# An attention-and-gate kernel on one core: TensorE's order for batches 1 to 3 written by slots, and batch 0's first stage in two parts

## Chip, core and metric

The kernel runs on one core of a Trainium2 chip. The metric is the device time of one execution in microseconds (us); lower is better. The engines are TensorE (PE), VectorE (DVE), ScalarE (ACT), GpSimd (POOL) and SyncE (SP), the last of which here only issues loads. Each engine carries out its own row of instructions in order.

## What is computed

Two layers in a row, on x of 4 batches, 12800 positions and 128 channels, with 32 inducing vectors. All arrays are float32, the three weights float64 on the host's side, and cut to what matters the reference is:

```python
def mab(q, kv):                      # scale = 1 / sqrt(128)
    s = scale * (q @ kv.transpose(0, 2, 1))
    s = s - s.max(-1, keepdims=True)
    a = np.exp(s)
    a /= a.sum(-1, keepdims=True) + 1e-09
    return a @ kv
h = mab(I, x)                        # 32 x 128 a batch: every position of x is read
x = mab(x, h)                        # back to 12800 x 128
# then, with a causal convolution of 5 taps a channel:
gate = 1.0 / (1.0 + np.exp(-gate_pre))   # gate_pre[t] = sum_k conv_w[k] * x[t - 4 + k]
val = x @ w_val
return gate * val @ w_out
```

The second layer's output of `mab` is a mixture of only 32 rows of h. The kernel therefore multiplies h by the taps and by w_val once a batch, and gets gate and value straight from the attention weights.

## The kernel before

A batch is cut into seven units: six of 4 x 512 positions and one of 4 x 128, which is unit 0 in batch 0 and unit 6 in the others (`units`). Its work has two stages.

**Stage 1** makes h. For each unit a load brings xT (channels by positions); TensorE multiplies it by the inducing vectors (`a_mm`, L280, four column tiles side by side), VectorE takes the maximum (`a_max`, L284) and transposes the scores into the tile e (`a_tr`, L289). When all seven units are there, `p_ml` to `p_mc` (L294 to L313) make one maximum of them: VectorE, TensorE, VectorE, TensorE, VectorE in turn. Then come the subtraction (`a_sub`, L318), the exp (`a_exp`, L323), the sum z (`a_z`, L335 or L342) and the product h (`a_h`, L353), which needs x with positions first, the tile xk. Batches 1 to 3 load xk, subtract and sum on GpSimd. Batch 0 makes xk by TensorE transposes (`a_kt`, L256, 100 of them) and ACT copies (`a_ke`, L269), and subtracts on VectorE. `p_z` to `p_hq` make the h weights hq. From these `p_v` to `p_we` make, on TensorE and in some 15 small VectorE steps, the stacked weights wstk (float16 in two parts) and wo.

**Stage 2** makes the outputs, unit by unit: scores against hq (`b_mm`, L456, psum tile of one buffer, tag s), transposition, row maximum, subtraction on GpSimd, exp on ACT, sum, normalizing on GpSimd, transposition back (`b_tr` to `b_back`, L461 to L493). Then it splits into two float16 parts (`b_hi` on ACT, `b_lo` on GpSimd with the four positions before each strip, L499 to L511). The **gate** is 60 row-tiled matmuls into two psum tiles g0 and g1 of one buffer each (`c_gate`, through `strips`, L520), then two tanh on ACT (`c_tanh`, L531). The **value** is 12 more matmuls into the same two psum tiles (`c_val`); VectorE multiplies value and gate (`c_gv`, L541, twice a unit), TensorE multiplies by wo (`c_out`, L546, four a unit, psum tag o with two buffers), ACT copies out (`c_ev`, L553) and stores.

In batch 3 the value is issued in two halves, the first after the first tanh (`PAIRS`); in the other batches it is issued whole, after both.

**What sets the order.** The program is not written in order. `stage1` and `stage2` hand each step to a list (`Plan.add`) with an engine, a planned duration, a key and the steps it needs; `Plan.order` then takes again and again, on the engine whose best step can start first, the step of the lowest key among those that can start within SLACK (0.17 us) of the earliest. The keys are linear in unit and batch: KEY1 for stage-1 scores, KEYH for h, KEYP for the steps on h, and in `stage2` the unit's number, less KS for the steps ahead of the gate. The resulting rows are static; nothing is chosen on the chip. Loads are one chain on SP's queue: all xT loads of a batch, then all its xk loads (batch 0 has none of these), then the next batch. xT has 12 buffers, freed by `b_mm`; xk has four, freed by `a_h`. The three weights are loaded on ACT's queue (`weights`, L194 to L196).

## Time and profile before

| | before |
|---|---|
| median of three runs | 338.98 us (338.87 to 339.67) |
| the profiled execution | 338.89 us |
| its span, first to last instruction | 337.1 us |
| mean granted TensorE clock | 0.975 |
| TensorE busy | 313.0 us |
| outputs (L546), 128x512 | 192 matmul instructions, 629 ns each |
| gate and value (L520), 512 wide | 1728 matmuls, 375 ns each |
| SP's queue, xT loads of 1 MB | 24, median 10.8 us to landing |

A float32 matmul is two instructions in the trace, so one output is x2 and the four scores of a unit are x8; a group of row-tiled or column-tiled matmuls runs side by side, and the times of single instructions in it overlap. In a row of the timeline stand start, length, engine, line, operation, output, inputs, shapes and count, and in brackets the idle time before it with what ended it. The ends of matmuls are modelled, so I read TensorE's costs from start to start. Weight loads (PEld) have a row of their own.

### The profile page before, as it was taken

To read this page: it belongs to the slowest core of one execution; us is meant where nothing else is said; L and a number is where in the kernel's file an instruction comes from. 1 tells how busy PE (TensorE), PEld (TensorE's weight loads), DVE (VectorE), ACT (ScalarE), POOL (GpSimd) and SP (SyncE) were. 2 spreads that over 40 slices of the span, in tenths; PEclk is the share of its full clock that TensorE was granted. 3 is DMA by queue.
4 is the path that set the end of the run, shared out by engine and by line. 5 is a ranking of instruction groups with operands and counts; after the bars stand their busy time and mean duration, and the time that the engine had idled before them with its cause. 6 is when DMAs were issued, how large, how long until landed. Compare 5 with 4: busy or idle time off the path is not lost.

```text
span 337.1 us, 9075 instructions
## 1 busy us (share of the span) xinstructions
PE 313.0 (93%) x3874; PEld 136.3 (40%) x3874; DVE 207.6 (62%) x412; ACT 171.2 (51%) x270; POOL 148.4 (44%) x244
## 2 busy tenths in 40 slices
PE   2999787999599999999799999999999999999993
PEld 0767623334343333334334333444443443333341
DVE  1578587845348867962756797844557878643220
ACT  1458032655334553576364354675643655665562
POOL 0000048349753223689683126899640376551000
PEclk9999859999989999999999999999999999999997
DMA  7997096008991638929984659763333140333324
GB/s 297 419 416 305 7 384 269 33 0 325 420 405 40 221 126 287 422 104 365 386 318 184 249 185 379 267 253 142 126 126 124 64 189 33 126 125 122 125 116 172
DMA packets 11475, 72.96 MB, mean 216 GB/s; under 512 B 1285, under 2 KB 1578, under 8 KB 2986
## 3 DMA queue, kind: packets, MB, share of 16 engines
q1 hardware_dynamic: 7056, 45.88, 35.2%
q10 hardware_dynamic: 4378, 26.50, 19.8%
q8 instruction: 30, 0.49, 0.6%
q14 instruction: 11, 0.09, 0.1%
HBM read 46.16 MB, written 26.21 MB: 215 GB/s over the span
## 4 chain that ended last, share of the span: by engine, by line
PE 85%; DMA 6%; DVE 3%; ACT 2%; POOL 1%; issue 1%; SPq 0%; ACTq 0%; POOLq 0%
PE g L520 30%; PE o L546 27%; PE s L280 7%; PE s L456 7%; PE h L353 7%; DMA xT<-in_xt_dram 5%; PE gp L256 4%; DMA ind<-in_inducing_dram 1%; PE wt L441 1%; POOL hl L504 1%; ACT gt L531 1%; ACT os L553 0%; DVE z L481 0%; PE zp L335 0%; PE t L308 0%
## 5 line engine op out<-in xcount | busy, mean ns | idle before, releaser
L520 PE MATMUL g<-hl,wstk 32*128 32x512 f16 (+1 forms) x2016 | 110.3, 352 | 0.5 <-ACT gt L531 0.5
L546 PE MATMUL o<-gt,wo 128*128 128x512 f32 (+1 forms) x224 | 105.6, 582 | 1.1 <-ACT os L553 0.6
L541 DVE SCALAR_TENSOR_TENSOR gt<-gt,g 128x1024 f32<-128x1024 f32 (+1 forms) x56 | 59.5, 1098 | 44.2 <-PE g L520 44.0
L553 ACT COPY os<-o 128x512 f32<-128x512 f32 (+1 forms) x112 | 59.2, 541 | 53.6 <-PE o L546 53.0
L520 PEld LDWEIGHTS <-wstk 32*128 32x128 f16 x2016 | 45.9, 92 | 75.6 <-issue 35.3
L531 ACT ACTIVATE gt<-g,gsc 128x1024 f32<-128x1024 f32 (+1 forms) x56 | 54.2, 1018 | 39.4 <-PE g L520 39.4
L471 POOL TENSOR_TENSOR q<-q,m 128x512 f32<-128x512 f32 (+1 forms) x28 | 26.8, 955 | 74.3 <-DVE m L466 73.7
L546 PEld LDWEIGHTS o<-gt,wo 128*128 128x128 f32 x224 | 35.4, 190 | 49.9 <-issue 29.8
L488 POOL TENSOR_TENSOR q<-q,z 128x512 f32<-128x512 f32 (+1 forms) x28 | 26.8, 956 | 51.5 <-DVE z L483 39.0
L504 POOL TENSOR_TENSOR hl<-p,hl 128x512 f16<-128x512 f32 (+1 forms) x28 | 29.6, 1057 | 21.3 <-ACT hl L499 21.0
L280 PE MATMUL s<-xT,iw 128*32 128x512 f32 (+1 forms) x224 | 28.5, 587 | 8.3 <-DMA xT<-in_xt_dram 5.8
L456 PE MATMUL s<-xT,hq 128*32 128x512 f32 (+1 forms) x224 | 30.0, 610 | 1.6 <-DVE hq L384 1.2
L284 DVE TENSOR_REDUCE nm<-s 128x1 f32<-128x512 f32 (+1 forms) x28 | 17.6, 627 | 21.0 <-PE s L280 21.0
L353 PE MATMUL h<-xk,e 128*32 128x128 f32 x800 | 28.2, 281 | 0.0
L318 POOL TENSOR_TENSOR e<-e,mb 128x512 f32<-128x512 f32 (+1 forms) x21 | 24.1, 1156 | 7.7 <-DVE mb L313 6.8
L499 ACT CAST hl<-p 128x512 f16<-128x512 f32 (+1 forms) x28 | 16.1, 575 | 22.3 <-DVE p L493 20.5
L353 PEld LDWEIGHTS h<-xk,e 128*32 128x32 f32 x800 | 21.9, 112 | 12.6 <-issue 5.7
L476 ACT ACTIVATE q<-q 128x512 f32<-128x512 f32 (+1 forms) x28 | 16.4, 586 | 20.6 <-POOL q L471 20.1
L481 DVE TENSOR_REDUCE z<-q 128x16 f32<-128x512 f32 (+1 forms) x28 | 17.3, 616 | 12.2 <-ACT q L476 12.1
L461 DVE STREAM_TRANSPOSE q<-s 128x512 f32<-128x512 f32 (+1 forms) x28 | 18.1, 647 | 8.2 <-PE s L456 8.2
L493 DVE STREAM_TRANSPOSE p<-q 128x512 f32<-128x512 f32 (+1 forms) x28 | 17.9, 641 | 8.0 <-POOL q L488 7.8
L342 POOL TENSOR_TENSOR za<-za,e 128x512 f32<-128x512 f32 (+1 forms) x18 | 20.5, 1141 | 2.1 <-ACT e L323 1.7
(88 smaller groups left out, 210.5 us busy)
## 6 DMA issues: line engine op xcount, KB each, us to landing
xT<-in_xt_dram SPq DMA_DIRECT2D x24, 1024.0 KB, 10.8
out_dram<-os ACTq DMA_DIRECT2D x24, 1024.0 KB, 4.4
xk<-in_xk_dram SPq DMA_DIRECT2D x18, 1024.0 KB, 8.5
xT<-in_xt_dram SPq DMA_DIRECT2D x4, 256.0 KB, 3.2
out_dram<-os ACTq DMA_DIRECT2D x4, 256.0 KB, 2.2
xk<-in_xk_dram SPq DMA_DIRECT2D x3, 256.0 KB, 4.9
raw<-in_moe_w_val_dram ACTq DMA_DIRECT2D x1, 128.0 KB, 7.6
raw<-in_moe_w_out_dram ACTq DMA_DIRECT2D x1, 128.0 KB, 10.0
```

What stands on the lines that cost most here:

```text
L280: T.matmul(sc[M * g:M * g + M, :w], c_["iw"], x[:, w * g:w * g + w], start=True, stop=True, tile_position=(0, M * g))
L318: (V if MADE(b) else Gp).tensor_tensor(e[:, :n], e[:, :n], bat[b]["mb"].broadcast_to([P, n, M]), ALU.subtract)
L353: T.matmul(d["h"][M * s:M * s + M, :P], e[:, i, :], x[i], start=v == 0 and i < G, stop=v == NU - 1 and i >= n - G, tile_position=(0, M * s))
L456: T.matmul(sc[M * g:M * g + M, :w], bat[b]["hq"], x[:, w * g:w * g + w], start=True, stop=True, tile_position=(0, M * g))
L471: Gp.tensor_tensor(q[:, :n], q[:, :n], st[b, u, "m"][:, :n].broadcast_to([P, n, M]), ALU.subtract)
L488: Gp.tensor_tensor(q[:, :n], q[:, :n], st[b, u, "z"][:, :n].broadcast_to([P, n, M]), ALU.mult)
L504: Gp.tensor_tensor(h[:, 1, 4:4 + w], st[b, u, "p"][:, :w], h[:, 0, 4:4 + w], ALU.subtract)
L520: T.matmul(bank[g // 2][:, g % 2, :w], wst[s, wp, k, :], h[s, part, 4 - d:4 - d + w], start=first and i == 0, stop=last and i == 2, tile_p ...
L531: S.activation(t[:, :, :w], st[b, u, "g"][i][:, :, :w], AF.Tanh, scale=bat[b]["gsc"])
L541: V.scalar_tensor_tensor(t[:, :, :w], t[:, :, :w], 1.0, st[b, u, "g"][i][:, :, :w], ALU.add, ALU.mult)
L546: T.matmul(op[:, :w], bat[b]["wo"], st[b, u, g // 2, "t"][:, g % 2, :w], start=True, stop=True)
L553: S.copy(os[:, w * g:w * g + w], st[b, u, g, "o"][:, :w])
```

## The change

What it does, part by part:

- **TensorE's order from slot 7 on** (a slot is one unit's gate and what follows up to the next gate; slot = 7 x batch + unit). Tables give each step a slot: S1AT for stage-1 scores, HAT for h, S2AT for stage-2 scores, MAXAT, HQAT, PVAT and WTAT for the small steps, EARLY for how many outputs of the unit before stand ahead of the value. Within a slot the places are: gate; weight copies; stage-1 scores; stage-2 scores; h; early outputs; value; remaining outputs. `at` records them, and at the end every step is made to need the one ahead of it. Up to slot 6 the planner still chooses, with new keys from the same tables, a wider SLACK, and a planned price for leaving a shape (SHAPE, LEAVE, KEEP).
- **The value is issued whole in batch 3 too** (PAIRS is false).
- **Psum:** stage-1 scores always use tag o, so s serves stage-2 scores alone; some small tiles and the second weight copy of a batch move to o.
- **Batch 0's stage 1 in two parts:** units 1 to 4, then 5, 6 and 0. Each part has its own maximum, sum and h; the first is subtracted on GpSimd, the second on VectorE. The new functions q_f to q_hq scale and join the two.
- **Batch 0's units 5 and 6 load xk** in place of transposing (68 transposes stay).
- **Loads:** xT and xk become two chains that the planner weaves together; the weights go to the head of SP's queue.
- Batch 0's weight copies take two wider steps in place of three.

The core of the diff (the tables' numbers but for a few left out; the new functions q_z, q_rz, q_hs and q_hc are a few VectorE steps on 32 columns each):

```diff
 def PAIRS(b):
-    return b == 3
+    return False
 def TAG1(b, u):
-    return "o" if b == 0 or b == 1 and u < 2 else "s"
+    return "o"
+FIXED = 7
+HAT = {1: (4, 4, 4, 4, 5, 5, 5), 2: (8, 8, 9, 9, 10, 10, 10), 3: (15, 16, 16, 17, 17, 17, 17)}
-def MADE(b):
-    return b == 0
+PARTS = ((1, 2, 3, 4), (5, 6, 0))
+def MADE(b, u):
+    return b == 0 and u not in (5, 6)
...
-            e = free[t["eng"]]
+            e = free[t["eng"]] + (LEAVE[last[0]] if t["eng"] == "PE" and t["shape"] != last[0] else 0.0)
...
-        nc.scalar.dma_start(raw[:TAPS, 2, :], conv_w)
-        nc.scalar.dma_start(raw[:, 0, :], w_val)
-        nc.scalar.dma_start(raw[:, 1, :], w_out)
+        nc.sync.dma_start(raw[:TAPS, 2, :], conv_w)
+        nc.sync.dma_start(raw[:, 0, :], w_val)
+        nc.sync.dma_start(raw[:, 1, :], w_out)
...
-        (V if MADE(b) else Gp).tensor_tensor(e[:, :n], e[:, :n], bat[b]["mb"].broadcast_to([P, n, M]), ALU.subtract)
+        (V if b == 0 and k else Gp).tensor_tensor(e[:, :n], e[:, :n], bat[b]["mb", k].broadcast_to([P, n, M]), ALU.subtract)
...
+    def q_f(b):
+        d = bat[b]
+        f = d["f"] = scratch(b)[:, 2, :2 * M].rearrange("p (k j) -> p k j", k=2)
+        mx = scratch(b)[:, 2, 2 * M:3 * M]
+        V.tensor_tensor(mx, d["mb", 0][:, 0, :], d["mb", 1][:, 0, :], ALU.max)
+        for k in range(2):
+            V.tensor_tensor(f[:, k, :], d["mb", k][:, 0, :], mx, ALU.subtract)
+    def q_fe(b):
+        S.activation(bat[b]["f"], bat[b]["f"], AF.Exp)
+    def q_zm(b, k):
+        d = bat[b]
+        t = d["zt", k] = ps("t", TAGP(b), [P, 512])
+        T.matmul(t[:, :M], c_["onesm"], d["zl", k], start=True, stop=True)
+    def q_hm(b, k):
+        d = bat[b]
+        t = d["ht", k] = ps("t", TAGP(b), [P, 512])
+        T.matmul(t[:, :M], d["hs", k], c_["id4"], start=True, stop=True)
+    def q_hq(b):
+        d = bat[b]
+        hT = d["hT"] = sbt("hT", [P, 1, M])
+        V.tensor_tensor(hT[:, 0, :], d["ht", 1][:, :M], d["f"][:, 1, :], ALU.mult)
+        V.tensor_tensor(hT[:, 0, :], hT[:, 0, :], d["h0"], ALU.add)
...
-                lk = last = add("SP", l(w, 0.1, 2.55), b * NU + v, load_k, (b, u), deps=[last], alloc="xk", lat=2.0)
+                lk = lastK = add("SP", l(w, 0.1, 2.55), b * NU + v + 0.5, load_k, (b, u), deps=[lastK, lastT] if b < 2 else [lastK], alloc="xk", lat=4.5 if b else 2.0)
...
+            if b:
+                at(mm, S1AT[b][v], 2, v)
...
+                if b:
+                    at(h, HAT[b][v], 4, v)
...
+            at(ga, slot, 0, 0)
...
+            at(va[0], slot, 5, -1)
...
+                    at(o, slot + 1, 6 if 2 * i + g % 2 >= EARLY[slot + 1] else 4.5, g)
...
+    fixed = [i for where, i in sorted(prog) if where[0] >= FIXED]
+    for i, j in zip(fixed, fixed[1:]):
+        plan.after(j, i)
```

What this moves is seen in the engines' rows. First TensorE in slots 8 and 9, in batch 1, before: s are scores (from iw stage 1, from hq stage 2), h the product with xk, o outputs; the rows of gate and value stand where "..." is. From the end of slot 8's value to the end of slot 9:

```order
L546 MATMUL o<-gt,wo 128x512
L353 MATMUL h<-xk,e 32x128 x16
L456 MATMUL s_2095<-xT,hq 32x512 x4
L353 MATMUL h<-xk,e 32x128 x16
...
L353 MATMUL h<-xk,e 32x128 x16
L546 MATMUL o<-gt,wo 128x512 x2
...
L546 MATMUL o<-gt,wo 128x512 x2
L353 MATMUL h<-xk,e 32x128 x16
L280 MATMUL s_2284<-xT,iw 32x512 x4
L353 MATMUL h<-xk,e 32x128 x16
```

And TensorE after, from the end of slot 8's gate to the end of slot 9:

```order
L314 MATMUL s_2024<-xT,iw 32x512 x4
L549 MATMUL s_2032<-xT,hq 32x512 x4
L389 MATMUL h<-xk,e 32x128 x32
...
L639 MATMUL o<-gt,wo 128x512 x4
...
L549 MATMUL s_2197<-xT,hq 32x512 x4
L389 MATMUL h<-xk,e 32x128 x32
...
L639 MATMUL o<-gt,wo 128x512 x4
```

A slot now has one run of scores and h and one of four outputs, where before it had outputs and h in turn, in smaller runs on both sides of the value.

Second, the start of SP's queue before (xT and xk are loads of the two layouts of x):

```order
L239 DMA xT<-in_xt_dram 128x2048 x6
L239 DMA xT<-in_xt_dram 128x512
L239 DMA xT<-in_xt_dram 128x2048 x6
L239 DMA xT<-in_xt_dram 128x512
L246 DMA xk<-in_xk_dram 128x2048 x6
L246 DMA xk<-in_xk_dram 128x512
```

And after:

```order
L228 DMA raw<-in_moe_conv_w_dram 5x128
L229 DMA raw<-in_moe_w_val_dram 128x128
L230 DMA raw<-in_moe_w_out_dram 128x128
L273 DMA xT<-in_xt_dram 128x2048 x6
L273 DMA xT<-in_xt_dram 128x512
L280 DMA xk<-in_xk_dram 128x2048 x2
L273 DMA xT<-in_xt_dram 128x2048 x6
L273 DMA xT<-in_xt_dram 128x512
L280 DMA xk<-in_xk_dram 128x2048 x4
L273 DMA xT<-in_xt_dram 128x2048 x2
```

The weights (raw) stand ahead of all xT, two xk loads come in for batch 0, and batch 2's first xT loads stand between batch 1's xk loads.

More of the change, by code (lines that the diff above doesn't have):

```diff
@@ L78, in add @@
         t = dict(i=len(self.tasks), eng=eng, dur=dur, key=key, fn=fn, args=args, deps=set(deps) | set(uses), alloc=alloc,
-                 users=[], lat=lat, start=None, end=None)
+                 users=[], lat=lat, shape=SHAPE.get(fn.__name__, "full"), start=None, end=None)
         t["users"].append(t["i"])
@@ L124, in order @@
             for eng, ids in ready.items():
-                c = [(earliest(T[i]), T[i]["key"], i) for i in ids]
+                c = [(earliest(T[i]), T[i]["key"] - (KEEP if eng == "PE" and T[i]["shape"] == last[0] else 0.0), i) for i in ids]
                 c = [x for x in c if x[0] is not None]
@@ L137, in order @@
             free[t["eng"]] = t["end"]
+            if t["eng"] == "PE":
+                last[0] = t["shape"]
             ready[t["eng"]].discard(i)
@@ L271, in a_ke, with a_mm @@
             V.tensor_copy(o, i)
-    def a_mm(b, u):
+    def a_mm(b, u, v):
         w = units(b)[u][1]
@@ L323, in a_exp, with a_z @@
         S.activation(e[:, :n], e[:, :n], AF.Exp)
-    def a_z(b, u, v):
+    def a_z(b, u, v, k=0, first=False, last=False):
         n = units(b)[u][1] // M
@@ L329, in a_z @@
         d = bat[b]
[L330 to L333 removed]
+        if b == 0:
+            if "zp" not in d:
+                d["zp"] = ps("zp", "s", [P, 2, P])
+            m = n // G
             for s in range(G):
[L335 to L336 removed]
+                T.matmul(d["zp"][M * s:M * s + M, k, :m * M], c_["ones"][:, :M], e[:, m * s:m * s + m, :].rearrange("p i j -> p (i j)"),
+                         start=first, stop=last, tile_position=(0, M * s))
             return
@@ L342, in a_z, with a_h @@
             Gp.tensor_tensor(d["za"][:, :n], d["za"][:, :n], e[:, :n], ALU.add)
-    def a_h(b, u, v):
+    def a_h(b, u, v, k=0, first=False, last=False):
         n = units(b)[u][1] // M
         d = bat[b]
-        if v == 0:
-            d["h"] = ps("h", "x", [P, 512])
+        if "h" not in d:
+            d["h"] = ps("h", "x", [P, 2, P])
         e = st[b, u, "e"]
@@ L574, in tile_kernel, with at @@
     gps, ws = [], None
+    prog = []
+    def at(i, *where):
+        prog.append((where, i))
+        return i
     def l(w, a, full):
@@ L579, in stage1 @@
     def stage1(b):
-        nonlocal last, ws
-        amax, atr, mms = [], [], []
-        lts = []
-        order = [(v + 1) % NU if b == 0 else v for v in range(NU)]
+        nonlocal lastT, lastK, ws
+        parts = PARTS if b == 0 else (tuple(range(NU)),)
+        order = [u for p in parts for u in p]
+        amax, atr = [], []
         kxs = {}
-        if MADE(b):
-            for u in order:
+        for u in order:
+            if MADE(b, u):
                 for k, (tag, n) in enumerate(HOME(u)):
```

298 lines of the change are left out of this document (184 added, 114 removed).

## The prediction

> **What bounds the kernel now.** I read the page first, then the busy time by stretches, then TensorE's timeline in three places. The page gives the span, the engines' shares and the chain that ended last:
>
> ```profile
> span 337.1 us, 9075 instructions
> PE 313.0 (93%) x3874; PEld 136.3 (40%) x3874; DVE 207.6 (62%) x412; ACT 171.2 (51%) x270; POOL 148.4 (44%) x244
> PEclk9999859999989999999999999999999999999997
> PE 85%; DMA 6%; DVE 3%; ACT 2%; POOL 1%; issue 1%; SPq 0%; ACTq 0%; POOLq 0%
> ```
>
> TensorE holds 85% of the chain at a full clock, except in one slice near 45 us and two near 90 us. I call the work from the start of one unit's gate (60 matmuls) to the start of the next a slot: slot 0 is batch 0's small unit, 1 to 6 the rest of batch 0, then seven to a batch, slot 27 the last small unit. These rows of the timeline open slots 1, 21 and 27, and the stretches 1 to 6, 7 to 20, 21 to 26 lie between them (stretch; length; busy time of PE, PEld, DVE, ACT, POOL):
>
> ```profile
> 55.89 3.42 PE L520 MATMUL g<-hl,wstk 32*128 32x512 f16 x60
> 274.47 3.42 PE L520 MATMUL g<-hl,wstk 32*128 32x512 f16 x60
> 326.16 1.03 PE L520 MATMUL g<-hl,wstk 32*128 32x128 f16 x60
> ```
>
> ```profile
> 55.89:130.51 74.62, 70.46 (x855) 28.45 (x851) 48.17 (x89) 34.86 (x53) 36.51 (x54) 0.98 0.49 190
> 130.51:274.47 143.96, 141.70 (x1829) 58.50 (x1829) 97.46 (x192) 80.19 (x129) 83.79 (x129) 1.00 0.60 231
> 274.47:326.16 51.69, 51.42 (x504) 19.10 (x504) 25.93 (x40) 29.00 (x47) 19.36 (x40) 1.00 0.27 107
> ```
>
> TensorE idles 4.2, 2.3 and 0.3 us in them: what shortens the kernel there must make TensorE's own work shorter. Its idle time is mostly two waits for loads, after the first of which it also runs slowly for a while:
>
> ```profile
> 90.82 1.56 PE L280 MATMUL s<-xT,iw 128*32 128x512 f32 x8 [3.57 <-DMA xT<-in_xt_dram]
> 164.63 1.07 PE L280 MATMUL s<-xT,iw 128*32 128x512 f32 x8 [2.19 <-DMA xT<-in_xt_dram]
> ```
>
> **The price of a run.** TensorE's matmuls have three shapes here: column tiles (scores, h), row tiles (gate, value, weight copies), and the whole array (outputs, transposes). One slot and a bit of batch 0, and a later run of three outputs:
>
> ```profile
> 119.39 3.42 PE L520 MATMUL g<-hl,wstk 32*128 32x512 f16 x60
> 122.74 1.07 PE L280 MATMUL s<-xT,iw 128*32 128x512 f32 x8
> 123.73 1.98 PE L546 MATMUL o<-gt,wo 128*128 128x512 f32 x4
> 125.65 1.07 PE L456 MATMUL s<-xT,hq 128*32 128x512 f32 x8
> 126.65 0.83 PE L520 MATMUL g<-hl,wstk 32*128 32x512 f16 x12
> 127.40 1.13 PE L546 MATMUL o<-gt,wo 128*128 128x512 f32 x2
> 128.46 1.06 PE L280 MATMUL s<-xT,iw 128*32 128x512 f32 x8
> ...
> 186.16 2.93 PE L546 MATMUL o<-gt,wo 128*128 128x512 f32 x6
> 189.02 3.42 PE L520 MATMUL g<-hl,wstk 32*128 32x512 f16 x60
> ```
>
> From start to start, one output costs 1.06, two 1.92, three 2.86. So an output is 0.86 and a run of them 0.20 more; the third adds 0.94, and I allow a third and fourth 0.1 together. A score matmul costs 1.00 alone; it streams the same 512 columns as an output, so I take 0.86 for it and 0.135 for its run. A gate costs 3.35 and a value 0.75: the 48 matmuls between them make 2.60, so twelve cost 0.65, and 0.1 of each is for its run. The four small units of 128 columns cost a quarter. With these prices the order of before adds up to 140.1 for slots 7 to 20 (125.0 of work, 15.1 for 99 runs) against 141.70 measured, so the prices hold to 1.6.
>
> [...]
>
> **Slots 7 to 20.** The new order has 61 runs there in place of 99: 2 row runs, 17 column runs and 19 output runs fewer. That is 0.2 + 2.3 + 3.8 = 6.3. Counted in the order, these slots also hold four stage-2 scores fewer, one stage-1 score and half an output more: 2.2 less. So 140.1 becomes 131.6. Three additions. First, the 1.6 that the prices miss. Second, 1.0 for ten fuller output runs. Third, a ring that the trace shows in the last batch, in a slot with no score in it:
>
> ```profile
> 282.90 3.42 PE L520 MATMUL g<-hl,wstk 32*128 32x512 f16 x60
> 286.26 1.98 PE L546 MATMUL o<-gt,wo 128*128 128x512 f32 x4
> 286.37 2.11 ACT L531 ACTIVATE gt<-g,gsc 128x1024 f32<-128x1024 f32 x2
> 288.17 1.18 PE L520 MATMUL g<-hl,wstk 32*128 32x512 f16 x12
> 289.10 2.35 DVE L541 SCALAR_TENSOR_TENSOR gt<-gt,g 128x1024 f32<-128x1024 f32 x2 [2.73 <-PE g L520]
> 291.50 3.43 PE L520 MATMUL g<-hl,wstk 32*128 32x512 f16 x60
> ```
>
> The gate's two banks are single. Gate, two tanh, value, and two products on VectorE follow one another, and only then may the next gate write. Batch 3 has the value in two halves, the first of which starts after one tanh, and its ring took 8.60. With the value whole, as the change makes it, the ring is 3.36 + 0.11 + 2.11 + 0.05 + 0.75 + 0.15 + 2.35 = 8.9, and no slot with full units can be shorter. From gate to value at least 2.27 pass. The new slot 7 has only 1.22 of scores there (1.1 lost), slot 14 falls under the ring (1.3), slot 15 loses 0.2: 2.6 together. Stage-1 scores now always take the outputs' two banks; the matmuls and the value that stand between a score and the next output cover VectorE's two readings of it, so I cost that at nothing; without that cover an output would wait about one reading more. The load wait at 164 us goes: SP's queue no longer holds the next batch's xT behind all seven xk, and the two are interleaved as buffers come free; each load that TensorE needs in these slots is issued at least one slot (9 us) before. The sum is 131.6 + 1.6 + 1.0 + 2.6 = 136.8, against 143.96.
>
> **Slots 1 to 6.** Before, the order prices at 67.5 against 70.46 busy; about 1.6 of the rest is the slow clock after the wait at 90 us. The new order has 32 runs in place of 48: 1 row, 6 column, 9 output runs fewer, 2.7, and one output less, 0.9. So 63.9; with the residue of 1.4 and 0.2 for the ring, 65.5 against 74.62. The 3.57 wait falls away for the same reason as above. What could be late next is GpSimd, which subtracts and sums for batch 1 in these slots beside six units of stage 2. Its work before was 36.51 of 74.62, so it has cover.
>
> **Slots 21 to 26.** Here the change costs. Slot 21 is bound by the ring, 8.9. Slot 22 has two stage-2 scores in a row in the one bank "s"; the second waits for VectorE's transposition of the first, for which I allow 0.8, so gate, scores, value and four outputs take 3.36 + 1.0 + 0.8 + 0.95 + 0.75 + 3.74 = 10.6. Slot 23 has 3.36 + 2.27 + 0.75 + 2.86 = 9.2. Slots 24 to 26 take the ring, 26.7. That is 55.4 against 51.69.
>
> **Up to slot 1.** Rows of the start:
>
> ```profile
> 0.75 12.75 SPq L239 DMA_DIRECT2D xT<-in_xt_dram  x11
> 1.89 0.27 DVE L193 MEMSET raw<- 128x256 int32 x1
> 3.11 0.48 ACTq L196 DMA_DIRECT2D raw<-in_moe_w_out_dram  x1
> 6.54 1.93 PE L280 MATMUL s<-xT,iw 128*32 128x512 f32 x8 [0.28 <-DVE iw L200]
> ```
>
> ```profile
> 24.66 2.08 PE L256 MATMUL gp<-identf,xT 128*128 128x128 f32 x16
> 28.96 1.92 PE L280 MATMUL s<-xT,iw 128*32 128x512 f32 x16
> 30.70 1.08 PE L353 MATMUL h<-xk,e 128*32 128x128 f32 x32
> 40.41 0.66 PE L456 MATMUL s<-xT,hq 128*32 128x128 f32 x8 [1.21 <-DVE hq L384]
> 41.84 0.40 POOL L471 TENSOR_TENSOR q<-q,m 128x128 f32<-128x128 f32 x1 [40.52 <-DVE m L466]
> ```
>
> The three weight loads move from ACT's queue to the head of SP's, where they wait for VectorE's memset (done at 2.16), and all xT loads are queued behind them. Three issues of some 0.45 put the first xT at 3.6 in place of 0.75. The first scores were not waiting for xT at 6.54, so the delay costs 0 to 2.8; I take 2.0. [...] Against the delay, 32 of 100 transposes go at 0.125 each (2.0 for 16), 4.0. Units 5 and 6 are loaded as xk instead; h needs them only after 30 us. Parting stage 1 lets GpSimd, idle for 40 us, subtract four units early; h then no longer waits behind two batch-1 scores for VectorE and ACT (28.96 to 30.70), 1.7. The second maximum and the joining of the halves cost 0.3 net. The first stage-2 scores come at 40.4 + 2.0 - 4.0 - 1.7 + 0.3 = 37.0. From there to slot 1 it was 15.5; VectorE's reading of a further batch-1 score ahead of unit 1 adds 1.0. The other edits there (a second constant, doubled small tiles, wider weight copies, ladder steps at other places in VectorE's row) lie beside TensorE's transposes and cost nothing. Slot 1 opens at 53.5, bounds 51 and 57, against 55.89.
>
> **The sum.** 53.5 + 65.5 + 136.8 + 55.4 = 311.2 for slot 27, against 326.16. Slot 27 and the drain keep their 10.9: the span is 322.1. The profiled execution took 338.89, 1.8 over its span, and stands 0.1 below the median of 338.98. So 323.9; I say **324.0**, 4.4% less. The low end is 317 (slot 1 at 51, no fuller-run cost, residues half, ring 0.3 less a slot), the high end of this case alone 330 (slot 1 at 57, half a microsecond more in every second slot).
>
> **Rivals.** (1) Runs are free: the three prices come from what stood beside the runs, not from the change of shape. Then 2.7 and 6.3 are not gained: **333**. Against it, the prices fit two stretches to 1.6 of 142. Chance 0.07.
>
> (2) Evacuation paces the outputs. They have two banks, ACT empties one in 0.59, and an exp of 0.63 that stands between makes it 1.22, more than the 0.86 of an output:
>
> ```profile
> L553 ACT COPY os<-o 128x512 f32<-128x512 f32 x96 | 55.5, 586 | 51.7 <-PE o L546 51.7
> L476 ACT ACTIVATE q<-q 128x512 f32<-128x512 f32 x24 | 15.2, 631 | 11.7 <-POOL q L471 11.2 <-POOL hl L504 0.4
> ```
>
> A third and a fourth output would each wait 0.36, in some 14 slots, 9 more than I have: **333**. For it: a third output already costs 0.08 more. Chance 0.12.
>
> (3) **Slower.** The products on VectorE are held up by an earlier step in its row. VectorE runs in order; before, the sum of the exps waited for ACT up to 2.6:
>
> ```profile
> DVE z L481 <- ACT q L476: 12.1, 9, 2.6
> ```
>
> TensorE's order is now fixed, so a late product holds the next gate and all behind it, where before other matmuls stood there. Four outputs last 3.6 and two products 2.35 plus latency, so 1.1 is free and 1.5 lost each time. It makes the kernel slower than 339.9 from 11 of the 21 fixed slots on; in 14 of them: **345**. Against it: VectorE is busy 97 of 144 there, and stage 2 leads the gate by two to three slots. Chance 0.06.
>
> My forecast keeps 0.75. About 0.3% is what a measurement of this kernel can tell from no change. Rivals (1) and (2) are faster too; a third rival in only eight to eleven slots ends at no change. So faster 0.93, same 0.03, slower 0.04. The range is 317 to 334, which takes in both rivals at 333.
>
> **What would show it.** In the new profile: runs of four outputs at 3.7, TensorE's busy time about 297; slot 1 opening near 53.5, slot 7 near 119, slot 21 near 256, slot 27 near 311; no wait of an "s" matmul for xT after slot 1; slots 24 to 26 near 8.9 with TensorE waiting for VectorE's products. I am wrong in the runs' price if slots 8 to 12 stay above 11 on average, in the ring if slots 24 to 26 stay at 8.6 or less, and in the whole if TensorE's idle time between slots 7 and 21 exceeds 10.

## The result, and the profile after

The changed kernel takes 330.31 us (median of four runs, 328.97 to 332.14) against 338.93 for the kernel before on the same chip (338.82 to 339.67). The ratio is 0.977, 95% interval [0.974, 0.980]: faster, and inside the range, but the gain is 8.6 us where 14.9 was forecast. The profiled execution took 331.38. Three single runs among the experiments below took 509 to 1039 us and stand in none of the figures. The page of the changed kernel, the rows that answer to those of before:

```profile
span 329.6 us, 9027 instructions
PE 304.3 (92%) x3849; PEld 135.3 (41%) x3849; DVE 208.7 (63%) x423; ACT 166.9 (51%) x265; POOL 154.0 (47%) x248
PEclk9999759799999999999999999999999999999998
PE 87%; DVE 5%; ACT 3%; issue 2%; POOL 1%; DMA 1%; SPq 0%; POOLq 0%; DVEq 0%
```

TensorE still holds the chain. The three stretches, slots 1 to 6, 7 to 20 and 21 to 26, in the same columns as in the prediction:

```profile
60.09:126.17 66.08, 65.95 (x853) 28.05 (x850) 50.56 (x89) 34.30 (x54) 37.11 (x55) 0.99 0.69 260
126.17:263.71 137.54, 135.80 (x1806) 58.78 (x1803) 92.59 (x186) 79.21 (x125) 81.54 (x126) 1.00 0.55 210
263.71:318.10 54.39, 51.63 (x522) 19.95 (x523) 28.30 (x44) 30.17 (x47) 20.84 (x41) 1.00 0.26 103
```

| | before | forecast | after, profiled |
|---|---|---|---|
| slot 1 opens | 55.89 | 53.5 | 60.09 |
| slots 1 to 6 | 74.62 | 65.5 | 66.08 |
| slots 7 to 20 | 143.96 | 136.8 | 137.54 |
| slots 21 to 26 | 51.69 | 55.4 | 54.39 |
| slot 27 and the drain | 10.9 | 10.9 | 11.5 |
| span | 337.1 | 322.1 | 329.6 |

The order by slots did what was forecast. The start, which was to open slot 1 2.4 earlier, opened it 4.2 later. The outputs of slot 8 and all of slot 9 on TensorE's timeline show the new order:

```profile
144.43 3.79 PE L639 MATMUL o<-gt,wo 128*128 128x512 f32 x8
148.15 3.42 PE L613 MATMUL g<-hl,wstk 32*128 32x512 f16 x60
151.50 1.06 PE L549 MATMUL s<-xT,hq 128*32 128x512 f32 x8
152.39 1.93 PE L389 MATMUL h<-xk,e 128*32 128x128 f32 x64
154.25 0.83 PE L613 MATMUL g<-hl,wstk 32*128 32x512 f16 x12
155.01 3.79 PE L639 MATMUL o<-gt,wo 128*128 128x512 f32 x8
```

Gate, one run of column tiles, value, one run of four outputs (3.72 from start to start; 3.74 was forecast), and no idle time between. The start looks different:

```profile
9.11 1.93 PE L314 MATMUL s<-xT,iw 128*32 128x512 f32 x8 [6.10 <-DVE w L253]
...
28.42 1.06 PE L389 MATMUL h<-xk,e 128*32 128x128 f32 x32
...
35.56 0.22 PE L371 MATMUL zp<-e,ones 128*32 128x32 f32 x1 [1.26 <-issue]
...
38.15 1.93 PE L314 MATMUL s<-xT,iw 128*32 128x512 f32 x8
40.01 0.64 PE L458 MATMUL t<-id,sc 128*128 128x32 f32 x2
41.52 0.66 PE L549 MATMUL s<-xT,hq 128*32 128x128 f32 x8 [0.87 <-DVE hq L475]
...
58.23 1.93 PE L314 MATMUL s<-xT,iw 128*32 128x512 f32 x8 [2.53 <-DVE e L323]
60.09 4.12 PE L613 MATMUL g<-hl,wstk 32*128 32x512 f16 x60
```

From 38 to 47 us the granted clock was 0.50, and a score took 1.93 instead of 1.06; it was near half again from 58 to 61. (The first score, at 9.11, took 1.93 too, with a granted clock of 1.00.) The candidates to be told apart are in these rows: the first scores, 2.57 later than before (behind the weight loads; the row names a step of VectorE, but in nine other profiles with these loads ahead the wait ends with the load of xT); a wait of 1.26 that the profile ascribes to nothing; a batch-1 score ahead of the second h transposition; the slow clock from 38; and the wait for the outputs' banks, 2.53, ahead of gate 1.

### The profile page after: what moved, and what is told of

Same layout as the page of the kernel before. It is cut to its first block, busy times and chain, and to the rows that moved or that the text cites. A ratio compares the mean times of both kernels' runs of the same rounds, so it can differ in the third digit from the quotient of the medians.

```text
span 329.6 us, 9027 instructions
## 1 busy us (share of the span) xinstructions
PE 304.3 (92%) x3849; PEld 135.3 (41%) x3849; DVE 208.7 (63%) x423; ACT 166.9 (51%) x265; POOL 154.0 (47%) x248
## 4 chain that ended last, share of the span: by engine, by line
PE 87%; DVE 5%; ACT 3%; issue 2%; POOL 1%; DMA 1%; SPq 0%; POOLq 0%; DVEq 0%
PE g L613 32%; PE o L639 27%; PE s L314 8%; PE s L549 7%; PE h L389 7%; PE gp L290 3%; ACT gt L624 2%; DVE gt L634 2%; PE wt L533 1%; DMA raw<-in_moe_w_out_dram 1%; ACT os L646 1%; PE t L344 1%; PE zp L371 0%; PE t L480 0%; DVE z L574 0%
## 5 line engine op out<-in xcount | busy, mean ns | idle before, releaser
L613 PE MATMUL g<-hl,wstk 32*128 32x512 f16 (+1 forms) x2016 | 112.8, 354 | 4.4 <-ACT gt L624 2.7
L639 PE MATMUL o<-gt,wo 128*128 128x512 f32 (+1 forms) x224 | 100.2, 574 | 1.0 <-DVE gt L634 0.7
L613 PEld LDWEIGHTS <-wstk 32*128 32x128 f16 x2016 | 47.1, 93 | 81.9 <-issue 40.4
L354 POOL TENSOR_TENSOR e<-e,mb 128x512 f32<-128x512 f32 (+1 forms) x25 | 29.0, 1181 | 31.6 <-DVE mb L349 31.5
L314 PE MATMUL s<-xT,iw 128*32 128x512 f32 (+1 forms) x224 | 29.9, 637 | 9.3 <-DVE w L253 6.1
L549 PE MATMUL s<-xT,hq 128*32 128x512 f32 (+1 forms) x224 | 28.1, 575 | 2.1 <-DVE q L554 1.3
L389 PE MATMUL h<-xk,e 128*32 128x128 f32 x800 | 25.5, 275 | 0.2 <-DVE sc L408 0.2
```

The costliest lines, as they stand in the source:

```text
L314: T.matmul(sc[M * g:M * g + M, :w], c_["iw"], x[:, w * g:w * g + w], start=True, stop=True, tile_position=(0, M * g))
L354: (V if b == 0 and k else Gp).tensor_tensor(e[:, :n], e[:, :n], bat[b]["mb", k].broadcast_to([P, n, M]), ALU.subtract)
L389: T.matmul(d["h"][M * s:M * s + M, k, :], e[:, i, :], x[i], start=first and i < G, stop=last and i >= n - G, tile_position=(0, M * s))
L549: T.matmul(sc[M * g:M * g + M, :w], bat[b]["hq"], x[:, w * g:w * g + w], start=True, stop=True, tile_position=(0, M * g))
L613: T.matmul(bank[g // 2][:, g % 2, :w], wst[s, wp, k, :], h[s, part, 4 - d:4 - d + w], start=first and i == 0, stop=last and i == 2, tile_p ...
L639: T.matmul(op[:, :w], bat[b]["wo"], st[b, u, g // 2, "t"][:, g % 2, :w], start=True, stop=True)
```

## Experiments: the start, first round

My theory was that each of these waits is paid in full. The rival was that steps between the first stage-2 score and slot 1 set the end of the start whatever is mended ahead of them. All ratios are against the kernel before on the same chip.

**Weight loads back on ACT's queue.**

```diff
-        nc.sync.dma_start(raw[:TAPS, 2, :], conv_w)
+        nc.scalar.dma_start(raw[:TAPS, 2, :], conv_w)
...
```

> The changed kernel with one edit: the three weight loads go out on ACT's queue again, as before the change, so no xT load stands behind them. Reading of the late start (theory): in the changed kernel the first xT was issued at 3.62 us in place of 0.75 and the first scores came at 9.11 in place of 6.54; all of the start hangs on it. Then the first scores come at 6.5 to 6.8, slot 1 opens near 57.7 (60.09 less 2.4), the stretches behind it stay as they are, and the time is near 328 (330.3 less 2.4). Rival: the steps between the first stage-2 score and slot 1 (VectorE, the outputs' banks) set slot 1 whatever the loads do; then slot 1 stays at 59.5 or later and the time within 0.6 of 330.3.

Three runs of 331.3 to 332.9, ratio 0.981 [0.977, 0.985]: no gain, and slot 1 opened at 59.44, not at 57.7. TensorE's timeline of this run:

```profile
6.17 1.93 PE L314 MATMUL s<-xT,iw 128*32 128x512 f32 x8 [0.28 <-DVE iw L234]
...
17.53 1.06 PE L314 MATMUL s<-xT,iw 128*32 128x512 f32 x8 [3.50 <-DVE e L323]
...
43.31 0.43 PE L549 MATMUL s<-xT,hq 128*32 128x128 f32 x8 [1.10 <-DVE hq L475]
```

The first scores did come 2.9 earlier, and the third waits 3.50 for VectorE, whose row has the conversion of the weights ahead of its readings of the scores; the granted clock was 0.5 for a while behind that wait, from 18.5 to 22 us. The first stage-2 score came at 43.31, later than in the run of the result. The delay of xT is real, but it pays for weights that land by 6 us, which VectorE converts while TensorE waits.

**Batch 1's scores behind the weight copies.**

```diff
-            mm = add("PE", l(w, 0.22, 0.87), key, a_mm, (b, u, v), deps=[kiw, lt], uses=[lt], alloc=TAG1(b, u))
+            mm = add("PE", l(w, 0.22, 0.87), key, a_mm, (b, u, v), deps=[kiw, lt] + (wready[:1] if b == 1 and v else []), uses=[lt], alloc=TAG1(b, u))
```

> The changed kernel with one edit: batch 1's scores from the second on wait until batch 0's weight copies have been written, so that the two of them that stood ahead of those copies on TensorE (44.38 to 47.79, at a low clock) now come after. Theory: those two delay the weight copies, and VectorE, which stands in its row at the cast of the second copy, then takes unit 1's maximum only at 49.36; with the edit the copies start near 45.5, the maximum comes near 47.5, and slot 1 opens 1.5 to 2 earlier, near 58.3; the time is near 328.5. Rival: it is the wait for the outputs' banks ahead of gate 1 (2.53) that sets slot 1; three batch-1 scores now stand in slot 0, and slot 1 stays at 60 or comes later; the time is 330 to 331.

328.33 (327.28 to 329.70), ratio 0.970 [0.967, 0.974]; slot 1 opened at 57.55 in the profiled run, 2.5 earlier. By these numbers the theory holds; by the trace it does not. This run had the full clock up to 43 us, and so has the next one, in which the two scores stand ahead of the copies as in the changed kernel. The first stage-2 score and VectorE's maximum of unit 1, of this run and then of the next:

```profile
40.46 0.43 PE L549 MATMUL s<-xT,hq 128*32 128x128 f32 x8 [1.11 <-DVE hq L475]
46.69 0.67 DVE L559 TENSOR_REDUCE m<-q 128x16 f32<-128x512 f32 x1
```

```profile
39.91 0.43 PE L549 MATMUL s<-xT,hq 128*32 128x128 f32 x8 [1.10 <-DVE hq L475]
46.14 0.67 DVE L559 TENSOR_REDUCE m<-q 128x16 f32<-128x512 f32 x1
```

6.23 lie between them in both. At the full clock the two scores delay nothing; at half the clock they did, since the maximum came 7.84 after the score in the run of the result (49.36 less 41.52).

**Value in two halves in batch 3.**

```diff
 def PAIRS(b):
-    return False
+    return b == 3
```

> The changed kernel with one edit: batch 3 has its value in two halves again, as before the change. Theory: in slots 21 and 24 to 26 the ring (gate, tanh, value, products) sets the length; it was 8.60 with the halved value in the kernel before and 8.6 to 9.0 with the whole one here, so each of these slots loses 0.2 to 0.3 and the time is 0.8 to 1.2 less, near 329.3; TensorE's busy time does not fall. Rival: the ring does not bind, TensorE's own work does; then the slots stay as they are, and the time within 0.3 of 330.3.

327.92 (326.96 to 328.45), ratio 0.969 [0.966, 0.972]. The edit changes nothing ahead of slot 21, and yet slot 1 opened at 56.05 in place of 60.09, with the first stage-2 score at 39.91: the same order at another clock. From slot 1 to slot 27 this run took 258.1, the changed kernel 258.5 (both to the row where slot 27's gate goes on after its first matmuls). Only slot 21 is shorter. The changed kernel, then this one:

```profile
263.71 3.42 PE L613 MATMUL g<-hl,wstk 32*128 32x512 f16 x60
...
272.48 3.42 PE L613 MATMUL g<-hl,wstk 32*128 32x512 f16 x58 [0.35 <-DVE gt L634]
```

```profile
259.86 3.42 PE L613 MATMUL g<-hl,wstk 32*128 32x512 f16 x60
...
267.88 3.42 PE L613 MATMUL g<-hl,wstk 32*128 32x512 f16 x60
```

8.02 against 8.77; slots 24 to 26 kept their lengths, since two outputs stand between gate and value there and both tanh are done within 0.12 us of the value's start. The halves are worth 0.75 in one slot, not 0.3 in four.

**Batch 1's fourth and fifth score behind gate 1.**

```diff
-            mm = add("PE", l(w, 0.22, 0.87), key, a_mm, (b, u, v), deps=[kiw, lt], uses=[lt], alloc=TAG1(b, u))
+            mm = add("PE", l(w, 0.22, 0.87), key, a_mm, (b, u, v), deps=[kiw, lt] + (gates[1:2] if b == 1 and v > 2 else []), uses=[lt], alloc=TAG1(b, u))
...
             at(ga, slot, 0, 0)
+            gates.append(ga)
```

> The changed kernel with one edit: batch 1's fourth and fifth score, which stood in slot 0 and waited 0.72 and 2.53 us for the outputs' banks, come after gate 1. Theory: unit 1's hl was ready at 59.06, so gate 1 can gain only 1.0 by it (slot 1 opens near 59.1), and the two scores cost 2.0 in slots 1 to 3: the time is near 331.3, a little longer. Rival: the banks' wait is what sets slot 1, since VectorE's readings of these two scores stand ahead of unit 1's steps; then slot 1 opens at 57 or before, and the time is 329.5 or less.

331.7 to 334.8 in three runs, ratio 0.982 [0.977, 0.986]: longer, as the theory had it. Slot 1 opened at 58.58, only 1.5 earlier: ahead of it small outputs now wait 4.62 for VectorE's products. Slots 1 to 3 took 37.8 in place of 33.2: the two scores, waits of 1.8 for products, and a slower clock under gate 1 (5.13 in place of 4.06). The banks' wait of 2.53 mostly lies beside the wait for unit 1's hl, which in the run of the result was written at 59.06, 1.0 before gate 1.

## Experiments: the price of a run and the order

**The shapes alone.** A program of TensorE matmuls in the kernel's shapes; it does not compute the reference.

```diff
+        def section(a, b, n):
+            for _ in range(n):
+                a()
+                b()
+            for _ in range(n):
+                a()
+            for _ in range(n):
+                b()
...
+        section(output, score, 12)
+        section(output, gate, 5)
+        section(score, gate, 5)
+        section(output, value, 10)
+        section(score, value, 10)
```

> Not the reference's computation: TensorE alone, on tiles filled with one number, with the matmul shapes of the kernel (an output of 128x128 by 512; a score of four column tiles by 512; a gate of 60 and a value of 12 row tiles by 512). Each pair of kinds is issued first in alternation, then the same matmuls again in two runs: 12 outputs and 12 scores, 5 outputs and 5 gates, 5 scores and 5 gates, 10 outputs and 10 values, 10 scores and 10 values. Theory (a run costs 0.20 for outputs, 0.135 for scores, 0.11 for gate or value): the alternation is longer than the two runs by 11 x 0.335 = 3.7, 4 x 0.31 = 1.2, 4 x 0.245 = 1.0, 9 x 0.31 = 2.8 and 9 x 0.245 = 2.2 us. Rival (runs are free): the two halves of each pair take the same time within 0.2 us.

The first section's last pair in alternation, then its two runs and the first row of the next section:

```profile
39.59 1.13 PE L213 MATMUL o<-gt,wo 128*128 128x512 f32 x2
40.64 1.07 PE L210 MATMUL s<-xT,iw 128*32 128x512 f32 x8
41.64 10.57 PE L213 MATMUL o<-gt,wo 128*128 128x512 f32 x24
52.14 10.51 PE L210 MATMUL s<-xT,iw 128*32 128x512 f32 x96
62.57 1.12 PE L213 MATMUL o<-gt,wo 128*128 128x512 f32 x2
```

A pair in alternation takes 2.05; twelve pairs in two runs 62.57 - 41.64 = 20.93, 1.74 a pair. Over 11 changes the difference is 3.7, as expected; the other four sections differ by 1.23, 0.99, 2.77 and 2.23 (expected 1.2, 1.0, 2.8, 2.2). Solved for the three shapes: **0.20** for a run of outputs, **0.14** for scores, **0.11** for gate or value. The first rival is refuted.

**The changed kernel without its order by slots.**

```diff
-FIXED = 7
+FIXED = 99
...
-LEAVE = dict(col=0.135, row=0.11, full=0.2)
-KEEP = 0.62
+LEAVE = dict(col=0.0, row=0.0, full=0.0)
+KEEP = 0.0
```

> The changed kernel without its order by slots: the planner lays down TensorE's order by its keys alone, with no price for a change of shape and no preference for the shape that runs; the start, the tiles and the loads' order stay. TensorE's order then has 81 runs in slots 7 to 20 in place of 61, and 39 in slots 1 to 6 in place of 32. Theory: at the prices of the prediction slots 7 to 20 come to 2.3 us more and slots 1 to 6 to 3.5 us more (of it 3.3 and 1.3 for runs, the rest work that moves between the stretches); with the waits of an order that VectorE's row no longer fits, the stretch from slot 1 to slot 27 is 5 to 9 longer and the time 335 to 340. Rival (runs are free and the gain came from the loads that are interleaved): that stretch is within 1.5 of the 258.5 of the changed kernel.

340.22 (339.3 to 343.01), ratio 1.006 [1.004, 1.009]: all of the gain goes, and a little more. From slot 1 to slot 27 it takes 273.3, 14.8 more than the 258.5 of the changed kernel. The three stretches of this run:

```profile
58.68:133.33 74.65, 72.49 (x871) 29.74 (x871) 50.06 (x97) 35.49 (x56) 37.47 (x56) 0.97 0.63 242
133.33:273.32 139.99, 136.65 (x1799) 57.51 (x1794) 89.86 (x176) 78.24 (x125) 81.01 (x126) 1.00 0.54 204
273.32:331.95 58.63, 52.23 (x515) 19.42 (x516) 29.84 (x46) 30.57 (x49) 20.67 (x41) 1.00 0.27 109
```

TensorE is busy 261.4 in them against 253.6, and idle 11.9 against 4.9. So of the 14.8 about half is runs and work that stays, with 1.25 of it the slow clock under gate 1 (5.31 in place of 4.06); half is waits, above all outputs that wait for VectorE's products. The sum of these waits, and one of the products:

```profile
PE o L639 <- DVE gt L634: 7.2, 7, 1.5
```

```profile
319.08 2.35 DVE L634 SCALAR_TENSOR_TENSOR gt<-gt,g 128x1024 f32<-128x1024 f32 x2 [7.26 <-PE g L613]
```

VectorE was not late. For 6.0 of the 7.2 it had stood idle (0.64 to 7.26) until the value came, and the outputs that wait stand right behind the value of their own unit. My 5 to 9 was too low. The rival (the interleaved loads alone) falls: those loads are in this kernel too, and no score waits for xT after the first.

**Batch 0's stage 1 in one part.**

```diff
-PARTS = ((1, 2, 3, 4), (5, 6, 0))
+PARTS = ((1, 2, 3, 4, 5, 6, 0),)
...
             if b == 0:
+                a = x = add("PE", 0.4, key, p_h, (b,), deps=[hs[0], zs[0]], alloc=TAGP(b))
+                ph.append(a)
+                a = add("DVE", 0.95, key, p_hq, (b,), uses=[x])
+            elif False:
                 q = [0, 0]
...
```

> The changed kernel with batch 0's stage 1 in one part again (one maximum, all seven subtractions on VectorE, no joining of two halves); units 5 and 6 are still loaded as xk, the order by slots stays. Theory: h then starts about 2 us later, but the wait of 1.0 to 1.5 for unit 6's xk near 35 us goes into that delay and the joining (about 0.5) falls away: the first stage-2 score comes 0.5 to 1.0 later than at the same place of the changed kernel at full clock (39.91 in the last runs), the time is 0.5 to 1 longer. Rival (the prediction: the parting is worth 1.7 less 0.3): the first stage-2 score comes 1.4 later or more. Second rival: the parting costs more than it brings, and the score comes earlier.

331.25 (330.92 to 331.51), mean clock 0.981 to 0.983, ratio 0.979 [0.977, 0.980]. The first stage-2 score came at 42.31, 2.1 later than in the second profile of the changed kernel, shown below (40.20). But this profile has half the clock from 30.5 to 34 us, which that one has not, so up to 1.7 of the 2.1 may be clock. The better measure is the time: at a mean clock of 0.983 the changed kernel takes 329.1 to 329.2, this one 331.06. So the parting is worth about 2 us: the prediction's 1.7 less 0.3 was a little low, my 0.5 to 1 here was wrong.

**Weight loads on ACT's queue, their conversion later in VectorE's row.**

```diff
-    kd = add("SP", 1.2, -1000, weights, alloc="os", lat=2.5)
-    kf = add("DVE", 0.55, -93.5, f64, (0,), deps=[kiw], uses=[kd], alloc="os")
+    kd = add("DMA", 9.0, -1000, weights, alloc="os")
+    kf = add("DVE", 0.55, -94.5, f64, (0,), deps=[kiw], uses=[kd], alloc="os")
...
-    lastT = lastK = kd
+    lastT = lastK = k0
```

> As the run with the weight loads on ACT's queue, and the conversion steps of the weights stand in VectorE's row where they fit weights that land near 13 us, as in the kernel before. In that run the first scores came at 6.17, 2.9 earlier, but VectorE's row had the conversion ahead of its readings of the second score, and TensorE waited 3.50 for it. Theory: without that wait the start keeps the 2.9: first score near 6.2, first stage-2 score near 37.5 at full clock in place of 39.9, slot 1 opens near 53.5, the time is 2 to 3 less than the changed kernel's at the same clock, near 326.5. Rival: the loads' bandwidth takes it back (unit 6's xk lands no earlier than 33 us, after 8.5 MB at 0.42 MB/us and what is interleaved with them); then the first stage-2 score comes at 39 or later.

330.63 (329.5 to 331.44), ratio 0.976 [0.974, 0.979]: no gain over the changed kernel. Neither I nor the rival had what the timeline shows:

```profile
6.29 1.93 PE L314 MATMUL s<-xT,iw 128*32 128x512 f32 x8 [0.28 <-DVE iw L234]
...
27.79 0.43 PE L314 MATMUL s<-xT,iw 128*32 128x128 f32 x8 [2.94 <-DVE e L323]
...
42.18 0.43 PE L549 MATMUL s<-xT,hq 128*32 128x128 f32 x8 [1.10 <-DVE hq L475]
```

The conversion only moves: now the last unit's score waits 2.94 for VectorE, busy 9.1 of the 10 us from 20 to 30. The granted clock behind that wait was 0.5, from 29 to 35 us, and this too lengthens the way to 42.18; the two are not separated. I read it so: with 32 transposes gone from TensorE, VectorE is the bound up to the second maximum, unless it converts the weights before the first scores arrive. The place at the head of SP's queue buys that.

## Experiments: the clock

**The changed kernel again.** No edit.

> The changed kernel unchanged, beside the two that follow. Theory: the slots from 4 on repeat to 0.1 us, and runs differ only in the start, by the clock that TensorE is granted between 34 and 60 us: the times spread over 3 us, and the runs with the higher mean clock are the shorter ones (326.5 to 328 at 0.99, 331 to 332 at 0.976). Rival: the spread has another cause (the loads); then time and mean clock do not go together.

329.12 (327.99 to 331.62), ratio 0.973 [0.970, 0.976]. With the four runs before, ten runs of one program:

| mean granted clock | time, us | runs |
|---|---|---|
| 0.976 to 0.977 | 330.9 to 332.1 | 4 |
| 0.983 | 329.1 to 329.2 | 4 |
| 0.988 | 329.0 | 1 |
| 0.993 | 328.0 | 1 |

In these ten runs the time follows the clock. The kernel before had 0.974 to 0.980 in the seven runs beside the first experiments, at 337.3 to 339.1 us. The start of the run at 0.993:

```profile
8.78 1.93 PE L314 MATMUL s<-xT,iw 128*32 128x512 f32 x8 [5.81 <-DMA xT<-in_xt_dram]
...
28.43 1.06 PE L389 MATMUL h<-xk,e 128*32 128x128 f32 x32
...
35.32 0.22 PE L371 MATMUL zp<-e,ones 128*32 128x32 f32 x1 [1.00 <-issue]
...
37.71 1.04 PE L314 MATMUL s<-xT,iw 128*32 128x512 f32 x8
38.69 0.41 PE L458 MATMUL t<-id,sc 128*128 128x32 f32 x2
40.20 0.43 PE L549 MATMUL s<-xT,hq 128*32 128x128 f32 x8 [1.10 <-DVE hq L475]
...
55.66 4.85 PE L613 MATMUL g<-hl,wstk 32*128 32x512 f16 x60
```

The same h start to 0.01, a wait of 1.00 in place of 1.26, and no half clock until 54: slot 1 opens 4.4 earlier. The stretch from 40 to 50 us (last three columns: granted clock, DMA share, GB/s), first in the run of the result, then in this one:

```profile
40.00:50.00 10.00, 8.90 (x104) 3.49 (x101) 7.61 (x30) 1.52 (x3) 0.99 (x3) 0.60 0.69 259
```

```profile
40.00:50.00 10.00, 7.73 (x170) 3.45 (x170) 9.21 (x32) 3.20 (x7) 3.92 (x9) 1.00 0.81 301
```

**Waits filled with matmuls nobody reads.**

```diff
+    def fill(tag, *cols):
+        t = ps("fill", tag, [P, 512] if tag == "x" else [P, 2, 512])
...
+            T.matmul(t[:, :n], c_["identf"], st[0, 0, "xT"][:, :n], start=True, stop=True)
+
     def a_h(b, u, v, k=0, first=False, last=False):
+        if b == 0 and u == 6:
+            fill("g0", 512)
...
     def b_mm(b, u):
+        if b == u == 0:
+            fill("x", 256)
...
     def a_mm(b, u, v):
+        if b == 1 and v in (3, 4):
+            fill("x", *((256,), (512, 512))[v - 3])
```

> The changed kernel with five matmuls more, whose results nobody reads, where TensorE waited in the start: one of 512 columns ahead of unit 6's h (the wait for its xk, 1.0 to 1.5), one of 256 ahead of the first stage-2 score (1.1), one of 256 and two of 512 ahead of batch 1's fourth and fifth score (0.8 and 2.5). Theory: the waits are what lowers the granted clock some 2 to 4 us later; with them filled the clock stays at 1.0 from 12 us on, every run has a mean clock of 0.99 or more, slot 1 opens at 55 to 56 in the profiled run, and the time is 326 to 327.5 in all runs, 2 to 4 below the changed kernel's mean. Rival (the clock falls whatever TensorE does there): the clock is below 1.0 somewhere in 36 to 60 in the profile and the times spread over 2 us or more as before, plus 0.3 for matmuls that do not fit their waits.

327.89 (326.77 to 328.59), ratio 0.968 [0.965, 0.970], mean clock 0.997 to 0.999 in all six runs. Without them it was 0.976 to 0.993 in ten runs, so here work in the waits held the clock, and the rival falls. The time gained less than forecast. In the profiled run h started 0.9 later than in the second profile above, and the first filling matmul missed its wait and cost 1.06:

```profile
36.40 0.25 PE L373 MATMUL zp<-e,ones 128*32 128x32 f32 x2 [1.21 <-issue]
36.58 1.12 PE L386 MATMUL fill<-xT,identf 128*128 128x512 f32 x2
...
57.66 3.42 PE L625 MATMUL g<-hl,wstk 32*128 32x512 f16 x60
```

I had put it behind what I took for the wait for unit 6's xk. The wait is one matmul group earlier, at a matmul that needs no load.

**Filled, halved, and one score moved.**

```diff
-S2AT = [-2, -1, 0, 1, 2, 3, 4, 0, -2, 1, 5, 8, 9, 10, 11, 12, 13, 14, 16, 17, 18, 18, 19, 21, 22, 22, 23, 24]
+S2AT = [-2, -1, 0, 1, 2, 3, 4, 0, -2, 1, 5, 8, 9, 10, 11, 12, 13, 14, 16, 17, 18, 18, 19, 20, 21, 22, 23, 24]
```

> The changed kernel with the five filling matmuls, batch 3's value in two halves, and one stage-2 score of batch 3 moved from slot 22 to slot 20 (the two after it move up by a slot), so that no slot has two in a row in the one bank. Theory: the halves give 0.75 in slot 21 (measured in the run with them alone), the moved score costs 1.0 in slot 20 and gives 1.0 and the wait of 0.84 in slot 22; slots 20 to 22 take 22.9 in place of 24.55, and the time is 1.2 to 1.6 below that of the kernel with the filling matmuls alone, near 325. Rival: VectorE or GpSimd is late for the earlier score, and slot 20 or 21 takes the 0.84 back; then the gain is 0.4 to 0.7.

327.3 to 329.1, ratio 0.968 [0.966, 0.970]: the same as with the filling matmuls alone. Slots 20 to 22 took 24.3, not 22.9: slot 20 grew by 1.0, slot 21 lost 0.75, slot 22 lost 0.5 of the 1.84. So the move costs more than it brings, worse than the rival's 0.4 to 0.7. What holds slot 22 then are its two tanh: ACT runs them from 274.06 to 276.18, and the second half of the value starts at 276.23.

**Four filling matmuls and the halves.** The first `fill` left out, `S2AT` as in the changed kernel.

> The changed kernel with batch 3's value in two halves and four of the five filling matmuls: the one ahead of unit 6's h is left out. In the run with all five it came after the wait near 35 us (1.21), not in it, and cost 1.1 on the path. Theory (what follows the waits in 40 to 57 us decides the clock): the mean clock is 0.995 or more in all runs, slot 1 opens at 54.8 to 55.6 in the profiled run, and the time is 326 to 326.8 in all runs. Rival (the filling matmul right behind the wait at 35 us was what kept the clock up): the clock falls to one half in 37 to 48 in some runs, the mean clock goes down to 0.976 to 0.99 there, and the times spread from 326 to 330.

326.22 (324.85 to 329.04), ratio 0.965 [0.962, 0.968]: the fastest kernel of this study, 2.9 us below the changed kernel's second median (the kernel before took 338.75 beside it and 338.59 there). Five of six runs have a mean clock of 0.994 or more; one has 0.984 and took 329.04, so the rival has a share too: these four make the drop rarer, not impossible. In the profiled run the clock was 1.000, slot 1 opened at 54.51 and the span was 323.1.

## Why the prediction came out as it did

**The price of a run** was right, to 0.01 for each shape. **Slots 7 to 20** (136.8 forecast, 137.54) and **slots 1 to 6** (65.5, 66.08) followed from it; slots 8 to 12 took 10.8 on average, under the 11 that I had set as the mark. No stage-1 score waited for its load after slot 1. The residues I allowed were about right. TensorE's busy time was 304.3, not the 297 of the signs, and 300.0 in the second profile, which had less of the slow clock.

**Slots 21 to 26** came to 54.39 instead of 55.4. Slot 22 took 10.7 and its second score waited 0.84 (0.8 forecast). The **ring** was mis-sized: by the mark I set, slots 24 to 26 at 8.6 or less, it is wrong. They took 25.7 together, 8.55 each from first matmul to first matmul, not 8.9 (8.72 each from slot 24's start to the row where slot 27's gate goes on):

```profile
300.74 0.39 PE L613 MATMUL g<-hl,wstk 32*128 32x512 f16 x2
301.40 3.42 PE L613 MATMUL g<-hl,wstk 32*128 32x512 f16 x58 [0.28 <-DVE gt L634]
```

The next gate starts when the first of the two banks has been read by the first product, and then waits for the second product. The two products do not both lie on the ring.

**Up to slot 1** is the step that failed: 60.09, not 53.5, outside the bounds of 51 and 57 in the profiled run.

| | forecast | profiled run | second profile |
|---|---|---|---|
| first scores | 8.5 | 9.11 | 8.78 |
| h starts | 27.0 | 28.42 | 28.43 |
| first stage-2 score | 37.0 | 41.52 | 40.20 |
| slot 1 opens | 53.5 | 60.09 | 55.66 |

- Of the 6.6, 4.4 lies between the two profiles of one program: 0.3 is the longer unexplained wait, the rest the granted clock. The other three parts, read from the second profile, are 1.4, 1.8 and -1.0. I had kept the slow clock of before as it was (15.5 from the first stage-2 score to slot 1, and 1.0 more for VectorE); I also read that clock off too coarsely, since it was 0.5 from 40 to 50 us, in two slices of the page and not one. The new order has more of TensorE's work there, the batch-1 scores among it, and at half the clock it costs 18.6; at full clock it cost 15.5, 1.0 less than my 16.5.
- 1.4 is the way to h. "The first scores were not waiting for xT at 6.54, so the delay costs 0 to 2.8; I take 2.0" was low by 0.2 to 0.6. The other 0.8 to 1.2 is work that the first maximum (0.44 of TensorE's time) and the sums z (0.46) now put ahead of h.
- 1.8 (3.1 at the low clock) lies between h and the first stage-2 score, for which I had taken the 9.7 of before and 0.3. There are two items in it that I did not price: the batch-1 score ahead of the second h transposition (0.98; 1.86 at half clock) and the unexplained wait (1.00 to 1.26).
- The first-order argument on the weights, "the delay costs", counted the cost and not what it buys. Two experiments that undid it gained nothing, though both also show half the clock behind the new wait.

**The rivals.** Free runs: refuted twice. Evacuation that paces the outputs: a run of four takes 3.72, so no. Late products: TensorE idles 1.7 in slots 7 to 20, none of it for products, so no. The 7.2 without the order by slots is another mechanism: there VectorE mostly waited for the value, and not an earlier step in its row held the products.

**What stays open.** The wait that the profile ascribes to "issue". It comes after 346 matmul records in nine profiles of eight programs (0.99 to 1.52), and after 347 in two more (0.52 and 0.56), in one of them with other rows around it; the second run with the weights on ACT's queue does not have it. Such a wait also stands inside a gate (0.44 near 87 us in the first experiment, 0.63 at 83.45 us in the one with a score moved). It is not the load of xk: both of batch 0's had landed by 29 us. From 32 to 34 us, just ahead of it in the run of the result, one packet of an instruction queue (0.02 MB) was moved, and the loads filled the DMA engines all the while (share 1.01):

```profile
30.00:35.00 5.00, 4.10 (x150) 3.72 (x138) 0.80 (x4) 0.88 (x3) 0.00 (x0) 1.00 1.01 415
```

The change adds two loads of 1 MB there; before, the DMA share from 30 to 35 was 0.30 and no such wait stood there. That the wait has to do with the packet or with the loads is not shown: in the first experiment the wait of 1.35 lies from 37.1 to 38.4, where the DMA share was 0.03 and no such packet was moved, and the kernel before has two such packets from 32 to 36 us and no wait. No run isolated it, and the cause stays open.

## What to carry to other kernels

Where TensorE is the bound, count the changes of shape in its order and price them by alternating the kernel's own shapes in a small program (0.20, 0.14 and 0.11 us a run here). Grouping was worth having: of the 14.8 us lost without the order by slots about half was runs and work that stays. Outputs should not stand right behind the value whose products they need (7.2 us of waits in that run). A start with waits of a microsecond on TensorE had no fixed length here (slot 1 opened at 60.09 and at 55.66 us in two profiles of one program): look at the granted clock of several runs before blaming an edit, and do not compare single profiles. Before undoing a load that "delays" the start, see which engine uses the delay (here VectorE, for which TensorE then waited 3.50 and 2.94 us).

## What was not expected of the hardware

The clock halved after a single wait of 1.26 us in the run of the result (1.00 during the wait, 0.50 from 38 to 47 us), and not each time: after the 1.35 in the first experiment it did not (the first stage-2 score took 0.43 there, 0.66 in the run of the result). The wait of 2.53 ahead of slot 1 had half the clock during it or right behind it in all seven profiles that have this wait (0.50 from 59 to 61 us in the run of the result; gate 1 took 4.85 in place of 3.42 in the second profile). Ten runs of one program spread from 327.99 to 332.14 us with mean clocks from 0.993 to 0.976, and five matmuls that nobody reads held it at 0.997 or more in six runs of six.
